# Sixths of the raw steps, halves of pair 0, and a swapped exponential: attention and a rational feed-forward layer on one core

## The chip, the core and the metric

The kernel runs on one core of one Trainium2 chip. A core has a matrix engine (PE, with its weight loads shown as PEld), a vector engine (DVE), a scalar engine (ACT), a general engine (POOL), an engine that issues most of the DMAs (SP), and 16 DMA engines. Each compute engine takes its own instructions strictly in order and waits on semaphores for the others. The metric is device microseconds (us) of one launch, the median over the runs; lower is better.

## What is computed

```python
scores = scale * q @ k.T                      # 4 batches x 12 heads, 448 tokens, head size 64, float32
scores = where(causal mask, scores, -1e9)
attn = exp(scores - rowmax);  attn /= sum(attn) + 1e-9
x = (attn @ v), heads side by side            # 1792 tokens x 768
h = x @ w_in                                  # w_in 768 x 2048, float64 in memory
g = (a0 + a1 h + a2 h^2 + a3 h^3) / (1 + |b0||h| + |b1| h^2 + 1e-6)
out = g @ w_out                               # w_out 2048 x 768, float64 in memory
```

The two weight matrices arrive as float64, so the kernel has to turn each 64-bit word into a float32 with integer operations.

## The kernel before

Two heads are handled together as one "pair"; there are 24 pairs, numbered 0 to 23, six to a batch. The loop over p runs from -1 to 23, and every turn works on several pairs at once: ORDER (lines 18 to 21) is a hand-written list of tasks, and `e.6@1` in it means task e, argument 6, for pair p-1. ORDER is the order in which instructions are put into each engine's queue. For one pair the tasks are: `ld` and `lv` (DMA loads of q, k and v, issued by SP), `qk` (PE transposes of q and k, line 296), `qx` and `qy` (copies of the two halves of rows out of PSUM, by ACT at line 311 and by DVE at 309 in the first pairs), `s` (scores, PE, line 328; s.0 makes block 0, and s.1, s.2 and s.3 make two blocks each), `m` (mask and row maximum, DVE, 339), `e` (exponential, ACT, 349; block 6 has 448 keys and block 0 has 64), `sm` and `r` (row sums on POOL, 356, reciprocal on DVE, 359), `n` (normalising, seven POOL operations, 366), `c` (PE transposes, 385), `a` and `v` (their copies by ACT, 395, and DVE, 397), `d` (attention times v, PE, 409), `dh` and `dl` (splitting the result into a high and a low part, ACT, and DVE at 437 or 439).

The conversion of weights is woven into this loop. A 128 x 768 piece ("raw" tile) m takes a POOL pass and then a DVE pass for each of two steps. In step 2, POOL copies the upper words (line 169, called by `cv.0`) and DVE shifts and ORs the lower words in (179). In step 3, POOL scales the upper words in place (173) and DVE shifts and ORs once more (185). `cv.0` stands near the start of a turn, behind POOL's last `n` of the turn before; the DVE pass, `cv.2`, stands at the end of a turn, behind DVE's last `m` and ahead of the `v` copies of the next turn. Before the change, pairs 3 to 15, 17, 19 and 21 each make one whole DVE pass of 768 columns (16 passes, eight pieces), with its POOL pass in the same turn. `quota` says how many steps a pair takes, and `conv` issues them.

At the start, matmuls on zeros (`keep_warm`, line 943, tile psI) fill PE until data come. After pair 23, a second hand-written list, TAIL, mixes the last attention work with the first feed-forward matmuls (`p1`, line 242, tile psH), whose PSUM banks are those of the closed score pool: the first psH tile takes the bank that pair 23's blocks 0 and 2 used. Then PE runs feed-forward work without a pause to the end. There too, DVE and POOL work side by side on weight pieces (lines 179, 185, 225, 525).

Of the kernel before, what the change touches and what calls it, by code (L numbers as in the profile page):

```python
# [17 lines left out]
ORDER = """  # L18
c.1@2 e.6@1 c.0@2 e.0@1 lv@-1 v.1@2 cv.0 dh@3 qk@-1 ld@-4 cv.3 a.1@2 sm@1 v.0@2 s.2 a.0@2 r@1 dl@3 qy@-1 n.2@1 s.3 qx@-1
n.3@1 m.3 m.4 s.0 n.5@1 s.1 e.3 m.5 d@2 n.0@1 e.4 n.4@1 m.0 e.5 m.1 n.6@1 m.2 e.1 m.6 n.1@1 e.2 cv.1 cv.2  # L20
# [7 lines left out]

FIRST = """
s.0 m.0 s.1 e.0 m.1 s.2 e.1 m.2 s.3 e.2 m.3 qk@-1 e.3 m.5 lv@-1 ld@-4 e.5 m.4 qy@-1 qx@-1 e.4 m.6 e.6  # L30
# [5 lines left out]
c.1@2 e.6@1 c.0@2 e.0@1 v.1@2 dh@3 a.1@2 xa.8 sm@1 xc.8.5 xa.9 v.0@2 a.0@2 r@1 co wl.0.0 xc.8.2 xc.8.3 xs.8 xd.11 xc.9.2  # L36
# [23 lines left out]
def kernel(  # L60
# [97 lines left out]
    def conv_step(m, s):  # L158
        raw = c_raw[m]
        yu = raw[:, :, 1]  # L160
# [11 lines left out]
        elif s == 5:  # L172
            nc.gpsimd.tensor_scalar(
                out=y, in0=y, scalar1=2.0 ** -112, scalar2=1.0, op0=ALU.mult, op1=ALU.mult
            )
        elif s == 4:
            nc.scalar.activation(out=y, in_=y, func=AF.Copy, scale=2.0 ** -112)
        elif s == 2:
            nc.vector.scalar_tensor_tensor(
                out=c_u[m], in0=raw[:, :, 0], scalar=29, in1=c_u[m],  # L180
                op0=ALU.logical_shift_right, op1=ALU.bitwise_or,
            )
        else:
            o = cv.tile([P, DM], F32, tag="ld", bufs=NL, name="w").bitcast(U32) if m < NL else c_u[m]
            nc.vector.scalar_tensor_tensor(
                out=o, in0=yu, scalar=3, in1=c_u[m], op0=ALU.logical_shift_left, op1=ALU.bitwise_or
            )
            c_32[m] = o.bitcast(F32)
# [65 lines left out]
    def stage_load(p):  # L254
# [33 lines left out]
    def qk_pe(p):  # L288
        ps = psa[p] = [ring(x, "psA") for x in range(2)]
# [9 lines left out]
        if p == 0:  # L299
            keep_warm(4)  # L300

    def qk_ev(p, x):
# [3 lines left out]
        o = QK[p].rearrange("p n (c r) -> p (n c) r", r=CP)[:, :, lo:hi]  # L306
        i = psa[p][x][:, :2 * NB * (hi - lo)].rearrange("p (c r) -> p c r", r=hi - lo)
# [139 lines left out]
    def conv(p, part):  # L447
        if part == 0:
            lo = sum(quota(x) for x in range(p))
            for m, n in steps[lo:lo + quota(p)]:  # L450
                conv_step(m, 1 if n == 2 else 5)
# [3 lines left out]
        else:  # L455
            lo = sum(quota(x) for x in range(p))
            mid, hi = lo + quota(p) // 2, lo + quota(p)
            for m, n in steps[lo:mid] if part == 1 else steps[mid:hi]:
                conv_step(m, n)
                if n == 3:  # L460
                    done.append(m)
# [3 lines left out]
        "qk": qk_pe, "qx": lambda p: qk_ev(p, 0), "qy": lambda p: qk_ev(p, 1),  # L465
# [5 lines left out]
    def parse(order):  # L471
# [9 lines left out]
        for order in (ORDER, FIRST, SECOND, THIRD)  # L481
# [411 lines left out]
    with tc.manual_schedule():  # L893
# [47 lines left out]
        def keep_warm(n):  # L941
            for _ in range(n):
                nc.tensor.matmul(idle, warm, warm, start=True, stop=True, skip_group_check=True)  # L943

        keep_warm(8)
# [6 lines left out]
        for p in range(NHEAD, NP):  # L952
# [4 lines left out]
            attend(p, begin[p] if 0 <= p < 3 else plan)  # L957
# [118 lines left out]
```

## Time and profile before

| What | Value |
|---|---|
| median of 3 runs | 602.48 us (602.44 to 602.89) |
| the profiled execution's own time | 602.94 us |
| its span, first to last instruction | 601.1 us |
| PE busy | 594.0 us, 99% of the span |
| DVE, ACT, POOL busy | 89%, 75%, 28% |
| chain that ended last: PE | 95% |

The span is what the trace shows, and the remaining 1.84 us lie around it. A busy engine in the table is one with an instruction in flight. The ends of matmuls are modelled, so that a PE that is busy all the time may still be held up a little by others. An instruction that waits inside the engine for something that is not a semaphore is shown as a longer instruction, not as idle time. So the length of a repeated stretch, and the length of one instruction beside its twins, tell more here than the busy shares.

### The profile page before, as it was taken

To read this page: it belongs to the slowest core of one execution; us is meant where nothing else is said; L and a number is where in the kernel's file an instruction comes from. 1 tells how busy PE (TensorE), PEld (TensorE's weight loads), DVE (VectorE), ACT (ScalarE), POOL (GpSimd) and SP (SyncE) were. 2 spreads that over 40 slices of the span, in tenths; PEclk is the share of its full clock that TensorE was granted. 3 is DMA by queue.
4 is the path that set the end of the run, shared out by engine and by line. 5 is a ranking of instruction groups with operands and counts; after the bars stand their busy time and mean duration, and the time that the engine had idled before them with its cause. 6 is when DMAs were issued, how large, how long until landed. Compare 5 with 4: busy or idle time off the path is not lost.

```text
span 601.1 us, 12762 instructions
## 1 busy us (share of the span) xinstructions
PE 594.0 (99%) x4660; PEld 494.2 (82%) x4660; DVE 535.9 (89%) x1015; ACT 448.6 (75%) x923; POOL 169.2 (28%) x266
## 2 busy tenths in 40 slices
PE   8999999999999999999999999999999999999997
PEld 6666666667888888888888888889999999998886
DVE  3999999988799999999999879998999999988950
ACT  4999999998877776668777776676477777677731
POOL 2899997766733401112333100000000000000000
PEclk9999999999999999999999999999999999999999
DMA  7979898776389988888985663443353344149872
GB/s 163 234 180 228 182 204 210 181 194 224 149 284 347 336 304 288 298 308 301 358 297 183 225 217 139 158 139 125 135 206 132 109 154 145 66 184 339 294 254 85
DMA packets 104863, 128.64 MB, mean 214 GB/s; under 512 B 70496, under 2 KB 82912, under 8 KB 104800
## 3 DMA queue, kind: packets, MB, share of 16 engines
q1 hardware_dynamic: 104800, 127.82, 67.2%
q8 instruction: 37, 0.61, 0.4%
q14 instruction: 26, 0.21, 0.1%
HBM read 98.31 MB, written 29.49 MB: 213 GB/s over the span
## 4 chain that ended last, share of the span: by engine, by line
PE 95%; DVE 2%; ACT 1%; POOL 1%; issue 0%; ACTq 0%
PE psO L614 25%; PE psH L242 22%; PE psQ L728 14%; PE psM L610 13%; PE psD L409 7%; PE psS L328 7%; PE psC L385 4%; PE psA L296 2%; PE psI L943 1%; ACT e L349 1%; POOL e L366 0%; DVE wq L707 0%; DVE xparts L637 0%; DVE p L528 0%; DVE at L397 0%
## 5 line engine op out<-in xcount | busy, mean ns | idle before, releaser
L614 PE MATMUL psO<-whl,gh 128*128 128x512 f32 x448 | 159.1, 391 | 0.0
L242 PE MATMUL psH<-xs,whl 128*128 128x512 f32 x576 | 136.7, 391 | 0.2 <-ACT e L349 0.2
L610 PE MATMUL psM<-whl,gh 128*128 128x256 f32 x448 | 126.2, 282 | 0.0
L242 PEld LDWEIGHTS psH<-xs,whl 128*128 128x128 f32 x576 | 105.9, 188 | 21.9 <-ACT e L349 0.3
L614 PEld LDWEIGHTS psO<-whl,gh 128*128 128x128 f32 x448 | 84.0, 188 | 17.8 <-ACT gh L540 0.4
L610 PEld LDWEIGHTS psM<-whl,gh 128*128 128x128 f32 x448 | 84.5, 189 | 1.7 <-DVE osb L598 0.3
L349 ACT ACTIVATE e<-psS,nm 128x448 f32<-128x448 f32 (+6 forms) x168 | 79.3, 568 | 4.3 <-DVE nm L339 3.2
L614 PE MATMUL psO<-whl,gl 128*128 128x512 f32 x224 | 81.1, 390 | 0.0
L728 PE MATMUL psQ<-xpart,wq 128*128 128x384 f32 x432 | 78.5, 336 | 0.1
L366 POOL TENSOR_SCALAR e<-e,r 128x192 f32<-128x192 f32 (+6 forms) x161 | 74.4, 487 | 13.9 <-DVE r L359 9.4
L728 PEld LDWEIGHTS psQ<-xpart,wq 128*128 128x128 f32 x432 | 74.8, 188 | 1.4 <-DVE hpair L754 0.4
L339 DVE CUSTOM_DVE_ANT_0 psS<-psS,mask 128x64 f32<-128x64 f32 (+6 forms) x168 | 65.4, 456 | 1.8 <-PE psS L328 1.3
L610 PE MATMUL psM<-whl,gl 128*128 128x256 f32 x224 | 63.2, 282 | 0.0
L169 POOL TENSOR_SCALAR u<-raw 128x768 f32<-128x768 f32 x32 | 36.9, 1153 | 57.6 <-DMA raw<-in_moe_w_out_dram 25.0
L517 ACT ACTIVATE w<-w 128x512 f32<-128x512 f32 x32 | 20.3, 633 | 39.8 <-DVE w L502 39.8
L614 PEld LDWEIGHTS psO<-whl,gl 128*128 128x128 f32 x224 | 42.0, 188 | 8.9
L328 PE MATMUL psS<-qkt 64*64 64x64 f32 (+6 forms) x672 | 47.5, 391 | 1.4 <-ACT e L349 1.2
L349 ACT ACTIVATION_READ_ACCUMULATOR e<-psS,nm 128x1 f32 x168 | 48.5, 299 | 0.0
L409 PE MATMUL psD<-at,vraw 128*64 128x448 f32 (+3 forms) x384 | 46.8, 386 | 0.0
L409 PEld LDWEIGHTS psD<-at,vraw 128*64 128x64 f32 x384 | 25.5, 136 | 24.9 <-issue 14.8
L610 PEld LDWEIGHTS psM<-whl,gl 128*128 128x128 f32 x224 | 42.3, 189 | 0.0
L328 PEld LDWEIGHTS psS<-qkt 64*64 64x64 f32 x672 | 21.3, 132 | 20.4 <-ACT at L395 10.7
(111 smaller groups left out, 1117.1 us busy)
## 6 DMA issues: line engine op xcount, KB each, us to landing
whl<-whl SPq DMA_DIRECT2D x64, 768.0 KB, 5.5
w<-w SPq DMA_DIRECT2D x51, 384.0 KB, 5.1
raw<-in_moe_w_in_dram SPq DMA_DIRECT2D x16, 768.0 KB, 5.4
raw<-in_moe_w_out_dram SPq DMA_DIRECT2D x16, 768.0 KB, 6.1
w<-u SPq DMA_DIRECT2D x26, 384.0 KB, 3.4
qraw<-in_q_dram SPq DMA_DIRECT2D x48, 112.0 KB, 3.5
kraw<-in_k_dram SPq DMA_DIRECT2D x48, 112.0 KB, 3.7
out_dram<-osb SPq DMA_DIRECT2D x13, 384.0 KB, 3.1
```

The costliest lines, as they stand in the source:

```text
L169: nc.gpsimd.tensor_scalar(out=u.bitcast(F32), in0=y, scalar1=0.0, scalar2=1.0, op0=ALU.mult, op1=ALU.mult)
L242: nc.tensor.matmul(ps, w[:, c * P:(c + 1) * P], xs[ck, part, c // K3][:, c % K3], start=(c == 0 and n == 0), stop=(c == KD - 1 and n == 2),)
L328: nc.tensor.matmul(pss[p, b][half((1 + b + j) % 2)], QK[p][half(j), 0, b * QB:(b + 1) * QB], QK[p][half(j), 1, :b_w[b]], start=True, stop= ...
L339: nc.vector.tensor_tensor_reduce(out=s, in0=s, in1=mask[:, S - w:], scale=-SCALE, scalar=3e38, op0=ALU.add, op1=ALU.min, accum_out=nmx[p][ ...
L349: nc.scalar.activation(out=E[p % 2][i][:, :w], in_=pss[p, i], func=AF.Exp, bias=nmx[p][:, i:i + 1], scale=-1.0, accum_out=SUM[p % 2][:, i: ...
L366: nc.gpsimd.tensor_scalar(out=e, in0=e, scalar1=REC[p][:, i:i + 1], scalar2=0.0, op0=ALU.mult, op1=ALU.add)
L385: nc.tensor.transpose(ps[x][:, slot // 2 * QB:(slot // 2 + 1) * QB], E[p % 2][n][r, lo:lo + P], ident[r, r])
L409: nc.tensor.matmul(ps[half(j), lo * QB:S], v[:, j, c], a[h][:, slot * QB:(slot + 7 - lo) * QB], start=(c == 0), stop=(c == 3), skip_group_ ...
L517: nc.scalar.activation(out=w, in_=w, func=AF.Abs)
L610: nc.tensor.matmul(acc["m", k], g, w[:, 512:], start=first and (k % 2 == 0 or each), stop=last, skip_group_check=True)
L614: nc.tensor.matmul(acc[k], g, w[:, :512], start=first, stop=last)
L728: nc.tensor.matmul(q_bank[j, bank], w[:, wp_, c * P:(c + 1) * P], xp_[:, c], start=(first and n == 0), stop=(n == 3 * K3 - 1), skip_group_ ...
```

## The change

It has three parts.

The raw steps are cut into sixths of 128 columns. A pair takes 5 sixths (pairs 3 to 12), 6 (13, 14, 15, 17, 19, 21), 4 (16) or 3 (18 and 20), 96 sixths in all for the same eight pieces. Sixths of the same step in one pair are joined into one DVE instruction, so a pair whose share crosses from one step into the next has two DVE instructions in a row where it had one. These are pairs 4, 5, 6, 7, 10, 11, 12, 13, 14, 15 and 19. POOL's pass is not cut: it is issued whole, at `cv.0` of the pair in which its step begins; only for the step that begins in pair 18 is it done by DVE, at `cv.2`, just ahead of that pair's 3 sixths.

Pair 0 is loaded, transposed and copied in two halves of 224 rows. The eight DMAs of q and k become halves, with q issued by SP and k by ACT; half 0 of both is transposed and copied, then block 0 of the scores is made, then half 1 is transposed and copied. The zero matmuls are 7 and, behind half 0, one of 128 and one of 64 columns, where there were 8, 2 and 4.

At the head of TAIL, the exponential of pair 23's block 0 (64 keys) is put ahead of that of block 6 (448 keys).

```diff
+ZEROTH = "lv@-1 qk.0@-1 ld@-4 qy.0@-1 qx.0@-1"
 FIRST = """
-s.0 m.0 s.1 e.0 m.1 s.2 e.1 m.2 s.3 e.2 m.3 qk@-1 ...
+s.0 m.0 qk.1 qx.1 qy.1 e.0 s.1 m.1 s.2 e.1 m.2 s.3 e.2 m.3 qk@-1 ...
 TAIL = """
-c.1@2 e.6@1 c.0@2 e.0@1 v.1@2 dh@3 a.1@2 ...
+c.1@2 e.0@1 c.0@2 e.6@1 v.1@2 dh@3 a.1@2 ...

-    def conv_step(m, s):
+    def conv_step(m, s, lo=0, hi=DM):
...
-        elif s == 5:
-            nc.gpsimd.tensor_scalar(
+        elif s in (5, 6):
+            (nc.gpsimd if s == 5 else nc.vector).tensor_scalar(
                 out=y, in0=y, scalar1=2.0 ** -112, scalar2=1.0, op0=ALU.mult, op1=ALU.mult
             )
...
-                out=c_u[m], in0=raw[:, :, 0], scalar=29, in1=c_u[m],
+                out=c_u[m][:, lo:hi], in0=raw[:, lo:hi, 0], scalar=29, in1=c_u[m][:, lo:hi],

     def stage_load(p):
...
-            for j in range(2):
-                nc.sync.dma_start(out=t[:, :, j], in_=src[b, 2 * hp + j].rearrange("(c p) d -> p c d", p=CP))
+            eng, nh = (nc.scalar if n == "k" else nc.sync, 2) if p == 0 else (nc.sync, 1)
+            for h in range(nh):
+                for j in range(2):
+                    x = src[b, 2 * hp + j].rearrange("(c p) d -> p c d", p=CP)
+                    cs = slice(h * NB // nh, (h + 1) * NB // nh)
+                    eng.dma_start(out=t[:, cs, j], in_=x[:, cs])

-    def qk_pe(p):
+    def qk_pe(p, h=None):
...
-            if p == 0 and n == 1:
-                keep_warm(2)
-            for c in range(NB):
+            for c in cols_of(h):
...
-        if p == 0:
-            keep_warm(4)
+        if h == 0:
+            keep_warm(1)
+            keep_warm(1, QB)

+    NQ = 6
     def quota(p):
-        return int(3 <= p < 16 or p in (17, 19, 21))
-    steps = [(m, n) for m in range(NC) for n in (2, 3)]
+        if 3 <= p < 13:
+            return 5
+        if p in (13, 14, 15, 17, 19, 21):
+            return 6
+        return {16: 4, 18: 3, 20: 3}.get(p, 0)
+    steps = [(m, n, i) for m in range(NC) for n in (2, 3) for i in range(NQ)]

     def conv(p, part):
+        now = steps[lo:lo + quota(p)]
         if part == 0:
+            for m, n, i in now:
+                if i == 0 and p != 18:
+                    conv_step(m, 1 if n == 2 else 5)
...
+        elif part == 2:
+            runs = {}
+            for m, n, i in now:
+                runs.setdefault((m, n), []).append(i)
+            for (m, n), r in runs.items():
+                if p == 18:
+                    conv_step(m, 6)
+                conv_step(m, n, r[0] * DM // NQ, (r[-1] + 1) * DM // NQ)

-        keep_warm(8)
+        keep_warm(7)
```

## Rows read from the trace of the kernel before

**Rows 1.** The page's part 1: busy us (share of the span) and instructions by engine.

```profile
PE 594.0 (99%) x4660; PEld 494.2 (82%) x4660; DVE 535.9 (89%) x1015; ACT 448.6 (75%) x923; POOL 169.2 (28%) x266
```

**Rows 2.** Busy time by stretch, one turn each: stretch, length, PE, PEld, DVE, ACT, POOL.

```profile
31.13:36.60 5.47, 5.47 (x95) 3.48 (x96) 5.47 (x20) 5.47 (x21) 4.98 (x10) 1.00 1.07 222
...
53.02:58.57 5.55, 5.55 (x94) 3.53 (x96) 5.55 (x22) 5.55 (x21) 5.05 (x10) 1.00 0.75 202
...
102.49:107.88 5.39, 5.39 (x94) 3.50 (x96) 5.33 (x20) 5.39 (x21) 3.33 (x9) 1.00 0.99 189
107.88:113.27 5.39, 5.39 (x94) 3.62 (x96) 4.47 (x20) 5.39 (x20) 4.38 (x10) 1.00 0.70 155
```

**Rows 3.** Timeline (start, length, engine, line, tiles): one split operation, then turn 10's end.

```profile
24.09 0.57 DVE L437 TENSOR_TENSOR xs<-psD,xs 128x448 fp32r<-128x448 f32 x1
...
65.82 1.08 DVE L185 SCALAR_TENSOR_TENSOR u<-raw,u 128x768 uint32<-128x768 uint32 x1
...
66.06 1.62 POOL L169 TENSOR_SCALAR u<-raw 128x768 f32<-128x768 f32 x1
...
68.13 0.64 DVE L437 TENSOR_TENSOR xs<-psD,xs 128x64 fp32r<-128x64 f32 x2
```

**Rows 4.** Timeline of DVE and POOL, where two DVE operations meet a POOL pass.

```profile
139.03 0.94 DVE L225 TENSOR_TENSOR whl<-w,whl 128x768 fp32r<-128x768 f32 x1
139.05 1.66 POOL L169 TENSOR_SCALAR u<-raw 128x768 f32<-128x768 f32 x1
139.89 1.63 DVE L179 SCALAR_TENSOR_TENSOR u<-raw,u 128x768 uint32<-128x768 uint32 x1
...
142.50 0.95 DVE L179 SCALAR_TENSOR_TENSOR u<-raw,u 128x768 uint32<-128x768 uint32 x1
```

**Rows 5.** Timeline around the end of turn 18, and a one-input DVE operation.

```profile
109.88 0.93 POOL L169 TENSOR_SCALAR u<-raw 128x768 f32<-128x768 f32 x1
...
110.47 1.29 DVE L397 COPY at<-psC 128x512 f32<-128x512 f32 x2 [0.92 <-PE psC L385]
...
131.10 0.56 DVE L217 CAST whl<-w 128x768 fp32r<-128x768 f32 x1
```

**Rows 6.** Timeline of the head.

```profile
0.74 0.93 SPq L262 DMA_DIRECT2D qraw<-in_q_dram  x2
...
1.11 3.78 PE L943 MATMUL psI<-e 128*128 128x128 f32 x16 [1.11 <-DVE e L939]
...
4.82 0.69 PE L296 MATMUL psA<-ident,qraw 64*128 64x64 f32 x8
...
5.44 1.22 PE L943 MATMUL psI<-e 128*128 128x128 f32 x4
...
7.31 0.59 ACT L311 COPY qkt<-psA 128x512 f32<-128x512 f32 x1 [5.30 <-PE psA L296]
...
8.51 1.95 PE L328 MATMUL psS<-qkt 64*64 64x64 f32 x28
...
10.53 0.57 DVE L339 CUSTOM_DVE_ANT_0 psS<-psS,mask 128x384 f32<-128x384 f32 x1 [0.24 <-PE psS L328]
```

**Rows 7.** The zero matmuls of two stretches: ns min/median/max, first and last start.

```profile
L943 PE MATMUL psI<-e x4: 421/421/580, 5.4 to 6.2; 128*128 128x128 f32 x4
...
L943 PE MATMUL psI<-e x6: 275/275/275, 7.5 to 8.1; 128*128 128x128 f32 x6
```

**Rows 8.** DMAs into qraw in the first 8 us: time from issue to landing.

```profile
DMA to landing us min/median/max: 2.4/3.2/3.5
```

**Rows 9.** Chain of waits, pieces in order of time (start, length, what): the head's end.

```profile
17.06 1.18 PE psC L385 x28
```

**Rows 10.** Timeline of the tail's begin.

```profile
136.71 0.66 ACT L349 ACTIVATE e<-psS,nm 128x448 f32<-128x448 f32 x1
...
137.32 0.34 ACT L349 ACTIVATE e<-psS,nm 128x64 f32<-128x64 f32 x1
...
137.80 3.97 PEld L242 LDWEIGHTS psH<-xs,whl 128*128 128x128 f32 x18 [0.31 <-ACT e L349]
```

More of the change, by code (lines that the diff above doesn't have):

```diff
@@ L286, in ring, with cols_of @@
         return (ps_s if n == 3 else ps_t).tile([P, 512], F32, tag=f"x{n}", name=name)
-    def qk_pe(p):
-        ps = psa[p] = [ring(x, "psA") for x in range(2)]
+    def cols_of(h):
+        return range(NB) if h is None else range(2 * h, 2 * h + 2)
+    def qk_pe(p, h=None):
+        if p not in psa:
+            psa[p] = [ring(x, "psA") for x in range(2)]
+        ps = psa[p]
         for n, src in enumerate(("q", "k")):
-            if p == 0 and n == 1:
-                keep_warm(2)
-            for c in range(NB):
+            for c in cols_of(h):
                 for x, w in enumerate((QB, CP - QB)):
@@ L305, in qk_ev @@
         lo, hi = x * QB, (QB, CP)[x]
-        o = QK[p].rearrange("p n (c r) -> p (n c) r", r=CP)[:, :, lo:hi]
-        i = psa[p][x][:, :2 * NB * (hi - lo)].rearrange("p (c r) -> p c r", r=hi - lo)
+        if h is None:
+            o = QK[p].rearrange("p n (c r) -> p (n c) r", r=CP)[:, :, lo:hi]
+            i = psa[p][x][:, :2 * NB * (hi - lo)].rearrange("p (c r) -> p c r", r=hi - lo)
+        else:
+            cs = slice(cols_of(h).start, cols_of(h).stop)
+            o = QK[p].rearrange("p n (c r) -> p n c r", r=CP)[:, :, cs, lo:hi]
+            i = psa[p][x][:, :2 * NB * (hi - lo)].rearrange("p (n c r) -> p n c r", n=2, r=hi - lo)[:, :, cs]
         if p == 3 or p < 3 and x == 1:
@@ L439, in d_lo @@
                 nc.vector.tensor_copy(out=o, in_=ps[:, r])
+    NQ = 6
     def quota(p):
-        return int(3 <= p < 16 or p in (17, 19, 21))
-    steps = [(m, n) for m in range(NC) for n in (2, 3)]
+        if 3 <= p < 13:
[4 more added lines that the diff above has]
+    steps = [(m, n, i) for m in range(NC) for n in (2, 3) for i in range(NQ)]
     done = []
     def conv(p, part):
+        lo = sum(quota(x) for x in range(p))
+        now = steps[lo:lo + quota(p)]
         if part == 0:
-            lo = sum(quota(x) for x in range(p))
-            for m, n in steps[lo:lo + quota(p)]:
-                conv_step(m, 1 if n == 2 else 5)
+            for m, n, i in now:
+                if i == 0 and p != 18:
+                    conv_step(m, 1 if n == 2 else 5)
         elif part == 3:
@@ L454, in conv @@
                 conv_load(done.pop(0) + NR)
[L455 to L460, printed above, removed]
+        elif part == 2:
[6 more added lines that the diff above has]
+                conv_step(m, n, r[0] * DM // NQ, (r[-1] + 1) * DM // NQ)
+                if n == 3 and r[-1] == NQ - 1:
                     done.append(m)
@@ L480 @@
         [(fn, arg, lag or 0) for fn, arg, lag in parse(order)]
-        for order in (ORDER, FIRST, SECOND, THIRD)
+        for order in (ORDER, ZEROTH, FIRST, SECOND, THIRD)
     )
@@ L939, with keep_warm @@
         nc.vector.memset(warm, 0.0)
-        def keep_warm(n):
+        def keep_warm(n, w=P):
             for _ in range(n):
-                nc.tensor.matmul(idle, warm, warm, start=True, stop=True, skip_group_check=True)
-        keep_warm(8)
+                nc.tensor.matmul(idle[:, :w], warm, warm[:, :w], start=True, stop=True, skip_group_check=True)
+        keep_warm(7)
         def attend(p, part):
```

22 lines of the change are left out of this document (12 added, 10 removed).

## The prediction

> **What bounds the kernel now.** I read the page's first part, then a table of the attention loop turn by turn, then timelines of DVE and POOL. PE is busy for 99% of the span [rows 1], so time can be won only where PE is held up: in the head, where little runs side by side; in turns that last longer than PE needs; and at the step into the feed-forward work. The reader should see in the table that turns 17 and 18 last 5.39 us, the one with a whole DVE pass in it and the other without [rows 2]. That is PE's own pace. Turns 3 to 14 last 5.44 to 5.55 us, and DVE is then busy all the time, as in turns 4 and 8 [rows 2]: there DVE is the bound. Over the 13 turns from 3 to 15 the excess over 5.39 adds up to some 1.5 us, which is all that a better spread could give back.
>
> The timeline of turn 10's end shows something that busy shares hide. DVE begins its pass at 65.82, POOL comes to its own pass at 66.06, and POOL's pass is 1.62 us long [rows 3], where one without a DVE pass beside it takes 0.93 [rows 5]. The two engines exclude each other. Later rows show the other side: DVE begins an operation on two SBUF operands at 139.03, POOL's pass comes up at 139.05, DVE's next such operation is due at 139.89 and takes 1.63 us, where a lone one takes 0.95 [rows 4]. So POOL waits for the first, then goes before the second, and the second waits 1.63 - 0.95 = 0.68 us. I counted ten places between 139 and 267 us where a POOL pass of this kind comes up under such a DVE operation with another right behind it; the second was lengthened in all ten, and no POOL pass waited for both. This decides the forecast, since the change puts two DVE passes in a row where there was one.
>
> The Trainium skill, in "SBUF — State Buffer", section "SBUF: two separate sides", has a rule that speaks against this change: DVE, when it reads two SBUF operands, and POOL, when it reads SBUF, share a pair of ports, and whoever starts first holds it for its whole instruction. By that rule the wait could be as long as the POOL pass itself, 0.93 us, and the sum below would be some 2.2 us higher. The trace agrees in kind, and its wait is 0.68.
>
> **The change part by part: the sixths.** Durations: cutting one DVE operation of 448 columns in two costs 0.64 - 0.57 = 0.07 us [rows 3], so I take 0.07 as the fixed part. A whole pass alone is 0.95 [rows 4]; a sixth is then (0.95 - 0.07) / 6 = 0.147. Five sixths cost 0.80 in one operation and 0.87 in two; six in two cost 1.02.
>
> Where DVE is the bound, its own sum is the turn. Turns 3, 8 and 9 take five in one operation: 0.15 less each, which brings 5.55 to about PE's 5.39 or 5.40, together -0.45. Turn 7 takes five in two, but turn 8 begins no step, so no POOL pass comes up: -0.08.
>
> Turns 4, 5, 6, 10, 11 and 12 take five in two, and 13 and 14 six in two, and in the turn behind each of these a step begins. Its POOL pass stands right behind POOL's last normalising operation, and that ends just after DVE's pass begins (65.82 against 66.06 [rows 3]; it is so in each of these turns). POOL's pass will therefore come up under the first of the two operations and go before the second: +0.68 each. Turns with five: 0.68 - 0.08 = +0.60, six times, 3.6. Turns with six: 0.68 + 0.07 = +0.75, twice, 1.5. Behind the waiting operation on DVE stand the `v` copies of the next turn, then `r`, `dl` and the `m`. PE's score matmuls wait for the banks that the `v` copies free, and the exponentials for `m`. In these turns DVE has no idle time that could take it.
>
> Turns 15 and 19 take six in two with no POOL pass behind: 0.07 each, partly in DVE's last slack, together +0.05. Turn 16's four sixths and turn 20's three fall into idle time of DVE. Turn 18 has 0.92 us of it, ahead of the copies [rows 5]. There DVE gets a scaling of 768 strided columns, priced between the 0.56 of a one-input operation of this size [rows 5] and the 0.95 of a two-input one [rows 4], half a pass (0.51), and the wait for POOL's pass between them, 0.68: 1.75 to 2.14, less 0.92, that is +0.8 to +1.2, and I take +1.0. What it takes away is a POOL pass of turn 18, which hid beside other work.
>
> Sum of this part: -0.45 - 0.08 + 3.6 + 1.5 + 0.05 + 1.0 = +5.6. Bounds: turns 4 and 10 have a first operation of one sixth only, 0.22 us, which may be over before POOL asks (-0.68 each), and turn 18 may cost nothing: +3.2. With waits as long as the POOL pass (0.93) in nine places it is +7.9.
>
> **The halves.** Eight zero matmuls took 3.78 us [rows 6], so seven end at about 4.4. Loads of q land 2.4 to 3.5 us after their issue, the median 3.2 [rows 8], and an SP issue takes 0.47 [rows 6]; half 0 of q and k, issued from 0.74 as two and two, lands by about 1.2 + 3.2 = 4.4, at the same moment. That ACT issues a DMA as fast as SP is not in the trace; if each took twice as long, half 0 would land near 5.4, +1.0. ACT's table load, now behind four issues, ends near 4.0, before its first copy. Eight transposes take 0.69 [rows 6]: 5.1. One and a half zero matmuls at 0.45 to 0.6 (two took 1.22 [rows 6]) end near 5.85, the shorter copies near 5.5, so block 0 starts at about 5.9 instead of 8.51. Eight more transposes: 6.75. Half 1's copies, shorter than the 0.59 of a whole one [rows 6]: 7.15. So s.2 starts at about 7.2. Before, all scores of pair 0 took 1.95 us [rows 6]; s.0 and s.1 are 384 of their 1792 columns, so s.2 started 0.42 behind 8.51, at 8.93. That is 1.7 earlier, and the same for the wait of DVE for the last scores, which ended at 10.53 [rows 6]. From there the chain runs through exponentials, sums and POOL to PE's first big transposes at 17.06 [rows 9] with the same steps as before: -1.7. Bounds: -2.6 if half 1 stays off the path, 0 if the clock (below) comes late.
>
> **The swap.** The first psH matmul starts at 137.80, its weight load having waited 0.31 for block 0's exponential, which started at 137.32 behind the one of 448 keys [rows 10]. In the new order it ends about 0.6 earlier, and PE is then held by its transposes: -0.25 (0 to -0.3). The row sums wait for both exponentials anyway.
>
> **Sum.** 602.94 + 5.6 - 1.7 - 0.25 = 606.6 for the profiled execution. The median of the runs shown is 0.46 below it, so I predict 606.1.
>
> **The rivals.** First, no turn is taken: the second DVE operation is already queued and follows at once. For it speaks that the two are short and of one kind; against it the ten places. Then turns 4, 5, 6, 10, 11 and 12 give 0.08 each, 13 and 14 cost 0.07 each, 18 about 0.3: -0.45 - 0.08 - 0.48 + 0.14 + 0.05 + 0.3 = -0.5, and with head and tail 602.48 - 2.45 = 600.0. This one ends on the other side, faster; it decides from the point where fewer than three or so of the nine waits happen. Second, the clock. The granted clock of the rows is 1.00 throughout, yet the zero matmuls' passes took 421 ns until 6.6 us and 275 ns from 7.2 on [rows 7], the lower and the higher of the two levels, 1.2 and 2.4 GHz; before the rise PE was fed without a gap from 1.11. The change takes out five and a half of 14 zero matmuls. If the rise came only behind pair 0's scores, s.1 to s.3 would take some 1.5 us longer and the head's gain would be 0.2: 607.6. The Trainium skill, in "TensorE: Matmul & The Clock Gate", Part 4, says that transposes don't bring the clock up, which leans that way; no row here separates it. Third, the waits come but fewer or shorter (turns 4 and 10 free, 18 cheap): 602.48 + 3.2 - 1.95 = 603.7, and lower if the first operation no longer waits for POOL: about 603.
>
> **How the numbers follow.** The forecast has 0.60 (606.1, its own range 604.0 to 607.8), no turn 0.20, the late clock 0.10, the few waits 0.10. A difference of 0.2%, 1.2 us, is about what a measurement of this kernel can tell from no change. Faster than 601.3: the first rival, 0.20. Within 0.2%: most of the third, 0.09. Slower than 603.7: the rest, 0.71. The range of 600.0 to 607.8 takes half of the first rival, all of the third and nearly all of the others.
>
> **What would show it.** In turns 4 to 6 and 10 to 14 the second of two DVE passes (lines for 179 and 185) should be about 0.7 us longer than its columns ask, with POOL's pass ending just before its end, and these turns should last 6.1 to 6.3 us, turns 3, 7, 8 and 9 about 5.4, turn 18 about 6.4. Block 0 should start near 5.9 and the first big transposes near 15.4. If the long passes are absent I was wrong about the turns; if block 0 starts near 5.9 but the transposes near 17, about the head.

## The result and the profile after

The changed kernel takes 608.01 us, median of 5 runs (607.68 to 609.27), beside 602.54 us (602.44 to 602.89) for the kernel before: a ratio of 1.010, 95% interval 1.0089 to 1.0112. (Ratios, here and below, are worked out over all runs of both kernels and need not be the quotient of the two medians.) It is slower, as forecast, by 1.9 us more than forecast and 0.2 us beyond the end of the range. The profiled execution took 608.01 us, with a span of 606.2 against 601.1.

The page's part 1 of the kernel after (busy us, share, instructions), which answers to [rows 1]:

```profile
PE 597.7 (99%) x4650; PEld 495.6 (82%) x4650; DVE 544.0 (90%) x1031; ACT 449.6 (74%) x924; POOL 168.2 (28%) x265
```

It hides everything: PE is 99% busy in both, though it does ten matmuls less. The turns tell more. Busy time by stretch of the kernel after, as in [rows 2], each stretch from one turn's first `psD` matmul to the next one's: turns 5, 6, 9, 11, 13 and 18.

```profile
35.70:41.82 6.12, 6.08 (x95) 3.80 (x93) 6.12 (x21) 5.56 (x19) 4.63 (x10) 1.00 0.62 136
41.82:47.97 6.15, 6.08 (x95) 3.81 (x93) 6.15 (x21) 5.56 (x19) 4.66 (x10) 1.00 0.64 144
...
59.34:64.86 5.52, 5.52 (x94) 3.48 (x92) 5.33 (x21) 5.52 (x21) 4.76 (x10) 1.00 1.04 261
...
70.51:76.64 6.13, 6.13 (x94) 3.80 (x92) 6.13 (x22) 5.62 (x20) 4.63 (x10) 1.00 0.77 168
...
82.80:89.08 6.28, 6.15 (x95) 3.81 (x93) 6.28 (x22) 5.62 (x20) 4.79 (x10) 1.00 0.87 186
...
112.14:118.03 5.89, 5.87 (x94) 3.66 (x93) 5.68 (x20) 5.07 (x19) 4.40 (x9) 1.00 0.61 128
```

Turns 5, 6, 11 and 12, with five sixths in two operations, last 6.12 to 6.16 us, and 13 and 14, with six, 6.27 to 6.28, where before they lasted about 5.5. The wait stands at the end of a turn and lengthens mostly the next one: the first of each run, turns 4 and 10, lasts 5.78 and 5.65, and turns 7 and 15, behind the last, still last 5.62 and 5.75. The timeline of DVE and POOL in the kernel after (start, length, engine, line) shows why: the ends of turns 4 and 11, and turn 18.

```profile
31.63 0.47 DVE L181 SCALAR_TENSOR_TENSOR u<-raw,u 128x128 uint32<-128x128 uint32 x1
31.92 0.96 POOL L171 TENSOR_SCALAR u<-raw 128x768 f32<-128x768 f32 x1
32.02 1.41 DVE L189 SCALAR_TENSOR_TENSOR w<-raw,u 128x512 uint32<-128x512 uint32 x1
...
72.66 0.54 DVE L181 SCALAR_TENSOR_TENSOR u<-raw,u 128x256 uint32<-128x256 uint32 x1
72.89 1.07 POOL L171 TENSOR_SCALAR u<-raw 128x768 f32<-128x768 f32 x1
73.12 1.26 DVE L189 SCALAR_TENSOR_TENSOR u<-raw,u 128x384 uint32<-128x384 uint32 x1
...
114.02 0.56 DVE L175 TENSOR_SCALAR raw<-raw 128x768 f32<-128x768 f32 x1
114.13 1.22 POOL L171 TENSOR_SCALAR u<-raw 128x768 f32<-128x768 f32 x1
114.61 1.15 DVE L189 SCALAR_TENSOR_TENSOR u<-raw,u 128x384 uint32<-128x384 uint32 x1
```

POOL's pass comes up under the first DVE operation, goes before the second, and the second is 1.41 us long. 512 columns alone take 0.68 (the fence of `e4_apart` below), so the wait is 0.73. It is the picture of [rows 4], and it stands in all nine places the forecast named, also where the first operation is one sixth, as at turn 4's end.

The head of the kernel after, answering to [rows 6, 9]: block 0's first scores, SyncE's issue of pair 3's `k`, its transposes, the first big transposes.

```profile
6.01 0.33 PE L345 MATMUL psS<-qkt 64*64 64x64 f32 x4
...
10.07 1.02 SPq L270 DMA_DIRECT2D kraw<-in_k_dram  x2
...
15.20 0.45 PE L307 MATMUL psA<-ident,kraw 64*128 64x64 f32 x8 [1.33 <-DMA kraw<-in_k_dram]
15.47 1.18 PE L402 MATMUL psC<-ident,e 64*128 64x64 f32 x32
```

Block 0 starts at 6.01 instead of 8.51. All 32 big transposes start at 15.47; before, four of them stood at 15.67 and 16.23, and 17.06 was the start of the other 28. But PE stands 1.33 us before pair 3's `k`. Two things come together there. The load is issued at 10.07, as before (10.02), since SyncE issues load after load without a pause from 0.74 us on. And it lands later, first in the kernel after, then in the one before:

```profile
DMA to landing us min/median/max: 4.5/4.6/4.7
DMA to landing us min/median/max: 2.9/3.0/3.1
```

In the kernel before, it had landed at 13.67 us. PE was ready for it at 13.87 in the kernel after (15.20 less 1.33), so with the landing time of before it would not have waited. The wait is handed on: DVE's copies of these transposes and POOL's normalising, which stands behind the reciprocal `r`, start 0.88 and 0.96 us earlier than before, not 1.7. After, then before:

```profile
15.69 1.16 DVE L326 COPY qkt<-psA 128x384 f32<-128x384 f32 x2 [0.63 <-PE psA L307]
18.24 3.19 POOL L383 TENSOR_SCALAR e<-e,r 128x192 f32<-128x192 f32 x7 [1.83 <-DVE r L376]
...
16.57 1.14 DVE L309 COPY qkt<-psA 128x384 f32<-128x384 f32 x2
19.20 3.21 POOL L366 TENSOR_SCALAR e<-e,r 128x192 f32<-128x192 f32 x7 [1.14 <-DVE r L359]
```

Why the load lands late isn't shown. Of the 19 traces of this document that issue it there, it took 3.6 us or more in nine, and these are the nine in which an instruction load of 0.02 MB begins at 12.54 us or earlier; in the ten in which that one begins later, it took 3.13 us or less. No run moves the instruction load.

The tail's begin, which answers to [rows 10]:

```profile
141.97 0.33 ACT L366 ACTIVATE e<-psS,nm 128x64 f32<-128x64 f32 x1
...
142.81 1.42 PE L246 MATMUL psH<-xs,whl 128*128 128x512 f32 x5
```

PE's wait of 0.31 us for the exponential is gone.

Below, "lead" is how much earlier a turn's first `psD` matmul starts than in the trace of before (20.05 us in turn 2, 25.51 in turn 3, and so on). After had a lead of 1.54 us in turn 2, 0.98 in turn 3, a lag of 0.50 in turn 7, 4.11 in turn 16, 5.28 in turn 21 and 5.01 in turn 25.

### The profile page after: what moved, and what is told of

Same layout as the page of the kernel before. It is cut to its first block, busy times and chain, and to the rows that moved or that the text cites. A ratio compares the mean times of both kernels' runs of the same rounds, so it can differ in the third digit from the quotient of the medians.

```text
span 606.2 us, 12764 instructions
## 1 busy us (share of the span) xinstructions
PE 597.7 (99%) x4650; PEld 495.6 (82%) x4650; DVE 544.0 (90%) x1031; ACT 449.6 (74%) x924; POOL 168.2 (28%) x265
## 4 chain that ended last, share of the span: by engine, by line
PE 83%; DVE 10%; issue 2%; ACT 2%; DVEq 0%; ACTq 0%
PE psO L642 25%; PE psH L246 22%; PE psQ L756 14%; PE psM L638 13%; PE psD L426 4%; PE psS L345 3%; DVE psS L356 3%; PE psC L402 2%; ACT e L366 1%; DVE at L414 1%; DVE u L181 1%; DVE nm L356 1%; PE psA L307 1%; DVE u L189 1%; DVE w L189 1%
## 5 line engine op out<-in xcount | busy, mean ns | idle before, releaser
L366 ACT ACTIVATE e<-psS,nm 128x448 f32<-128x448 f32 (+6 forms) x168 | 77.9, 509 | 9.5 <-DVE nm L356 5.2
L345 PE MATMUL psS<-qkt 64*64 64x192 f32 (+6 forms) x672 | 51.7, 391 | 1.5 <-ACT e L366 0.8
L345 PEld LDWEIGHTS psS<-qkt 64*64 64x64 f32 x672 | 23.9, 132 | 23.0 <-DVE at L414 8.6
L181 DVE SCALAR_TENSOR_TENSOR u<-raw,u 128x768 uint32<-128x768 uint32 (+5 forms) x39 | 41.8, 1071 | 0.0
```

The costliest lines, as they stand in the source:

```text
L181: nc.vector.scalar_tensor_tensor(out=c_u[m][:, lo:hi], in0=raw[:, lo:hi, 0], scalar=29, in1=c_u[m][:, lo:hi], op0=ALU.logical_shift_right, ...
L345: nc.tensor.matmul(pss[p, b][half((1 + b + j) % 2)], QK[p][half(j), 0, b * QB:(b + 1) * QB], QK[p][half(j), 1, :b_w[b]], start=True, stop= ...
L366: nc.scalar.activation(out=E[p % 2][i][:, :w], in_=pss[p, i], func=AF.Exp, bias=nmx[p][:, i:i + 1], scale=-1.0, accum_out=SUM[p % 2][:, i: ...
```

## The experiments

**The parts alone.** My theory: each place where two DVE passes follow each other with a POOL pass beside costs some 0.7 us, and the sixths are the whole loss. The halves alone (passes whole, old tail), the sixths alone, and the kernel before with every whole pass cut in two halves in its place:

```
# e1_halves: the changed kernel with
return 6 * int(3 <= p < 16 or p in (17, 19, 21))   # quota, and the old TAIL
# e2_sixths: the kernel before with conv_step, quota, steps and conv of the changed one
# e3_cut: the same, quota as in e1_halves, and in conv
-    conv_step(m, n, r[0] * DM // NQ, (r[-1] + 1) * DM // NQ)
+    for x in range(2):
+        conv_step(m, n, x * DM // 2, (x + 1) * DM // 2)
```

> Only the halves of pair 0 are added to the kernel before; the raw steps stay whole and the exponentials in their old order. Theory: half 0 and block 0 bring the head 1.6 us forward, and then pair 3's k, whose DMAs SP issues no earlier than before, holds PE up, so that about 1.0 us is left at turn 3 and kept to the end: 601.5 us (601.0 to 602.0). Rival, that the head's gain is given back later in turns that DVE bounds: 602.3 to 602.7. My prediction's own term, -1.7: 600.8.

> Only the sixths are added to the kernel before; head and tail are the old ones. Theory (POOL's pass takes its turn between two DVE operations in nine turns, 0.6 to 1.0 us each): 602.5 + 6.3 = 608.8 us (607.8 to 609.5), with the second operation of turns 4, 5, 6, 10 to 14 some 0.7 us longer than its columns ask. Rival, that the loss comes from the earlier head meeting later loads: near 603.

> The kernel before with its old shares, but each whole DVE pass of the raw steps in pairs 3 to 21 is cut into two of 384 columns, one right behind the other. Nothing else is changed, and no work is moved to another turn. Theory: in turns 3 to 14 a POOL pass comes up under the first and goes before the second, 0.68 + 0.07 us each, 12 times: 602.5 + 9.0 = 611.5 us (610 to 612.5), while turns 15, 17, 19 and 21, behind which no POOL pass follows, hardly change. Rival, that a cut costs only its fixed part and the loss came from where the sixths lie: 12 x 0.07 = 0.8 us, 603.3 us.

Measured beside 602.37 us for before: the sixths 609.14 us (ratio 1.0111, 1.0090 to 1.0133), the cut passes 611.46 (1.0148, 1.0128 to 1.0169), both as my theory had them; nothing is moved in `e3_cut`, and it is the slowest of the three. The halves took 603.52 (1.0019, 1.0009 to 1.0028), where I expected a gain: a miss, taken up below.

**The second operation elsewhere.** The changed kernel, with the second of two operations moved behind the `v` copies:

```
-sm@1 v.0@2 s.2
+sm@1 v.0@2 cv.4@1 s.2        # cv.2 issues the first operation, cv.4 the others
```

> The changed kernel, with the second DVE operation of a pair moved behind the two v copies of the next turn, which read PSUM; in pair 18 the half pass moves behind them too. The work is the same, only the place of the second operation differs, so that POOL's pass runs beside the copies. Theory: the second operations take no longer than their columns ask, turns 4 to 6 and 10 to 12 last 5.4 to 5.45 us, 13 and 14 about 5.6, turn 18 at most 0.5 more than 5.39: 601 us (600.3 to 602.3). Rival, that two operations cost as much wherever they stand, or that the copies' delay was not the path: 606 to 608 us.

604.36 us (1.0031, 1.0019 to 1.0042): most of the loss is gone, so it hung on the two operations standing together. But it is 3.4 us above what I expected. Timeline of turn 4's end in `e4_apart`:

```profile
31.74 0.49 DVE L181 SCALAR_TENSOR_TENSOR u<-raw,u 128x128 uint32<-128x128 uint32 x1
32.05 0.97 POOL L171 TENSOR_SCALAR u<-raw 128x768 f32<-128x768 f32 x1
32.57 1.29 DVE L414 COPY at<-psC 128x512 f32<-128x512 f32 x2 [0.34 <-PE psC L402]
...
33.77 0.68 DVE L189 SCALAR_TENSOR_TENSOR w<-raw,u 128x512 uint32<-128x512 uint32 x1
```

The DVE copies, which read PSUM, run beside POOL's pass without waiting, and the 512 columns take 0.68.

**Is it POOL's pass?** `e3_cut`, with POOL's exponent pass (every second turn's) shortened to 32 columns; the weights are not the reference's.

```
+    z = y[:, :32]
-    out=y, in0=y, scalar1=2.0 ** -112, ...
+    out=z, in0=z, scalar1=2.0 ** -112, ...
-    op0=ALU.logical_shift_left, ...      # step 3; unscaled values would overflow
+    op0=ALU.logical_shift_right, ...
```

> The kernel with every whole pass cut 3 + 3 (611.46 us), with GpSimd's exponent pass shortened from 768 columns to 32; GpSimd's other pass, in every second turn, keeps its 768. The shift of the third step goes right instead of left, for the same time, since unscaled values would overflow; the weights are not the reference's. My theory, a GpSimd pass that waits takes its turn between two VectorE operations and the second waits for it to end: the turns whose cut pass stands beside the short one fall from 6.3 to 5.5 or 5.6 us, the others stay at 6.3; 6 or 7 turns by 0.65 us, so 607.2 us (606.5 to 608.2). Rival, cutting a pass costs its 0.7 us whatever GpSimd does (the second operation must wait for the first one's writes, or for anything but GpSimd): all cut turns stay at 6.3 us and the time at 611.5.

607.31 us (1.0077, 1.0060 to 1.0095), as my theory had it. Timeline (start, length) of a turn with the long and of one with the short POOL pass, DVE's two operations in one row each:

```profile
43.99 1.92 DVE L188 SCALAR_TENSOR_TENSOR w<-raw,u 128x384 uint32<-128x384 uint32 x2
44.28 1.23 POOL L169 TENSOR_SCALAR u<-raw 128x768 f32<-128x768 f32 x1
...
50.27 1.22 DVE L180 SCALAR_TENSOR_TENSOR u<-raw,u 128x384 uint32<-128x384 uint32 x2
50.56 0.51 POOL L174 TENSOR_SCALAR raw<-raw 128x32 f32<-128x32 f32 x1
```

The two DVE operations take 1.92 us beside the long pass, 1.22 beside the short one, and the turns alternate, for instance these two:

```profile
41.95:48.18 6.23, 6.03 (x96) 3.81 (x92) 6.23 (x21) 5.54 (x19) 4.74 (x10) 1.00 0.65 156
48.18:53.80 5.62, 5.62 (x94) 3.99 (x92) 5.62 (x21) 5.58 (x20) 3.95 (x10) 1.00 1.19 248
```

So the price is POOL's pass, not the cut.

**The tail, the halves again, and earlier loads.** `e5_tail` is the kernel before with the new TAIL order alone; `e6_early_loads` is `e1_halves` with pair 3's loads ahead of pair 0's `v`:

```
-ZEROTH = "lv@-1 qk.0@-1 ld@-4 qy.0@-1 qx.0@-1"
+ZEROTH = "ld@-4 lv@-1 qk.0@-1 qy.0@-1 qx.0@-1"
```

> The kernel before with only the order of pair 23's two softmax pieces changed (64 keys ahead of the 448). My theory: the 0.33 us piece ends 0.6 us earlier than the 448 keys' did, and the wait of 0.2 to 0.3 us at the first column matmul goes: 602.37 - 0.2 = 602.2 us (602.0 to 602.4). Rival, the matmul has something else to wait for and nothing moves: 602.4. The trace's head is that of the kernel before, so it also shows how far that head varies from one execution to the next: block 0's first score matmul at 7.2 to 7.5 us as in the two kernels that cut the passes without the halves, or at 8.5 as in the profiled execution of before.

> The halves alone, a second time, as the control for the next kernel: 603.5 us (602.8 to 604.0). Its trace should show the first score matmul at 5.4 to 6.3 us and again a wait of about 1 us of pair 3's k transposes for their load, at 14 to 15 us; if its later turns wait for k loads too, as one did at 55 us in the first trace, then the gain is given back to the loads, and if they don't, something else makes this kernel's median longer.

> The halves alone, with pair 3's q and k issued ahead of pair 0's v on SyncE. Theory one, the head ends at pair 3's k, whose issue at 10.1 us stands behind pair 0's v: the issue comes at 8.2 us, the wait of 1.3 us at the k transposes goes, and the time falls by 0.9 us (0.5 to 1.3) against the halves alone, to about 602.6 us. Theory two, all loads of the first 60 us come at the pace of the DMA queues (engines 86% busy), so that what is moved ahead makes another load late: no change, 603.5 us, and a wait appears at pair 0's v or at a later pair's k.

The tail: 601.94 us beside 602.49 (0.9994, 0.9985 to 1.0004). Too little for the runs to tell from nothing, but in the trace the lead grows from 0.27 us in turn 23 to 0.53 in turn 24. The halves again: 602.76 (1.0002, 0.9989 to 1.0015). Earlier loads: 603.33 (1.0006, 0.9995 to 1.0018); pair 3's `k` transposes start at 13.93 us, and the next step, the big transposes, now waits for POOL: nothing gained, theory two by the time. In the trace, though, its lead of 1.39 us in turn 2 is kept (1.40 in turn 3), while the six traces with a long wait for this `k` lose 0.28 to 1.10 us there: in the head the wait did cost that, and the median doesn't show it.

In after, `e1_halves` both times, `e4`, `e6` and `e10` the halves' lead in turn 2 is 1.4 to 2.1 us, and it melts in three places: at pair 3's `k` (a wait of 0.9 to 1.5 us in six of the eleven traces with the new head: after, five of `e1_halves`, `e4`, `e6`, `e10`, `e12`, `e15`); at the first weights, for which POOL waits 0.2 to 1.6 us at 21 to 23 us in five traces with halves; and in turn 13, below. The old head is not free of the first two: `e2` and `e3`, the two of its traces that reach turn 2 earliest (18.78 and 18.96 us), wait 0.51 and 0.26 us for the weights and 0.35 and 0.41 for a `k`. So it may be the early head that meets these loads, not the halves as such; no run tests that.

**Another place for the pass.** `e9_behind` is `e5_tail` with the whole passes moved behind the `v` copies, where they shouldn't meet POOL's pass; `e10_behind_halves` adds the halves.

```
-ld@-4 cv.3 a.1@2 sm@1 v.0@2 s.2 ... n.1@1 e.2 cv.1 cv.2
+ld@-4 a.1@2 sm@1 v.0@2 cv.1@1 cv.2@1 cv.3 s.2 ... n.1@1 e.2
```

> The tail's change, and every whole VectorE pass moved from ahead of the copies of the transposed softmax to behind them, one turn later, so that it no longer stands beside GpSimd's pass. My theory: which of the two passes comes first decides, and behind the copies they do not meet, so GpSimd's pass takes 0.93 us instead of 1.62 in all turns and VectorE's never 1.72; turns fall from 5.5 towards the 5.39 of the turns without a pass, by 0 to 0.1 us in 13 turns: 602.4 - 0.25 - 0.6 = 601.5 us (600.8 to 602.3). Rival: the pass in its new place delays the masks of the next scores, as the second operation did where it stood behind the copies (turns 8 to 12 gained nothing, three others lost 0.3): 602.3 to 604 us.

> The same with the halves of pair 0. In the traces of the halves a lead of 1.1 to 1.8 us at pair 6 fell to 0.2 to 0.9 us, most of it in the turns after one in which GpSimd's pass came 0.01 to 0.3 us ahead of VectorE's, which then took 1.72 or 1.40 us instead of 1.07. Theory one, the halves' gain is lost to that order of the two passes: with the passes apart it stays, and this kernel is 1.1 us (0.8 to 1.5) below the one beside it, about 600.4 us. Theory two, the gain is lost to the loads of the first 60 us: within 0.4 us of the one beside it.

610.47 us beside 602.61 for before (1.0132, 1.0115 to 1.0149): a clear miss. The passes don't meet any more (0.95 and 0.93 us), but all turns with a pass last 6.0 us. Timeline of `e9_behind`, the lines of the kernel before:

```profile
39.84 1.29 DVE L397 COPY at<-psC 128x512 f32<-128x512 f32 x2 [0.55 <-PE psC L385]
41.05 0.95 DVE L179 SCALAR_TENSOR_TENSOR u<-raw,u 128x768 uint32<-128x768 uint32 x1
41.91 0.19 DVE L359 RECIPROCAL r<-r 128x7 f32<-128x7 f32 x1
42.28 0.89 POOL L366 TENSOR_SCALAR e<-e,r 128x192 f32<-128x192 f32 x2 [1.58 <-DVE r L359]
```

The reciprocal stands behind the pass, POOL waits 1.58 us for it, PE's big transposes wait for POOL, and DVE's copies for PE (0.55 us): a ring of 6.0 us. `e4_apart` put its second operation into the same place, and in its long turns, as 5 and 12, POOL waits up to 1.0 us for the reciprocal; its trace goes from a lead of 1.10 us in turn 3 to a lag of 0.82 in turn 25. That this is what it lacks is not shown; I have not tried it apart from that. `e10_behind_halves` took 610.81 (1.0136, 1.0120 to 1.0152), 0.34 above its neighbour, which is theory two by the time; its trace keeps a lead of 1.3 us over the other from turn 3 to the end, which is theory one. But the profiled run of `e10_behind_halves` is the fastest of its four (609.50) and that of `e9_behind` the slowest of its four (610.78), so the 1.3 us say little of the medians. Four runs don't settle it.

**Whole passes beside a short POOL pass,** without and with the halves (the edit of `e8_short_pool` on the kernel before and on `e1_halves`):

> The kernel before, passes whole and in their place, with GpSimd's exponent pass shortened from 768 columns to 32 (the weights are not the reference's; the third step shifts right for the same time). In the kernel before VectorE's pass comes first in all eleven turns, so the other's length costs nothing: 602.4 us (601.9 to 602.7). If the time falls by more than 0.5 us, GpSimd's pass is on the path in some executions of the kernel before too. It is the base of the next kernel.

> The halves alone, with the same short exponent pass: the turns where GpSimd's exponent pass came first (at 59 and 82 us in the traces of the halves) can no longer cost VectorE 0.3 to 0.7 us. Theory one, the halves' gain is lost to the order of the two passes: 0.9 us (0.5 to 1.5) below the kernel beside it. Theory two, it is lost at the loads (the wait of 1.0 to 1.3 us for pair 3's k and the later ones): within 0.4 us of it.

602.21 us (1.0001, 0.9991 to 1.0011) and 602.76 (1.0009, 0.9999 to 1.0019). The first fits: POOL's pass, when it comes second, is off the path. The second says that the order of the passes is not all. Its trace shows something else in the head. Timeline, pair 0's later scores in `e12_short_pool_halves`:

```profile
7.31 3.06 PE L345 MATMUL psS<-qkt 64*64 64x192 f32 x24
```

and in `e1_look4`:

```profile
6.19 2.15 PE L345 MATMUL psS<-qkt 64*64 64x192 f32 x24
```

The same 24 matmuls take 1.42 times as long in `e12_short_pool_halves`, as the zero matmuls of [rows 7] did before the rise (1.53 times), with a granted clock of 1.00 in the rows of both. The first transposes that run fast start at 10.30 us there, and turn 2's first `psD` is 0.58 us later than in `e11_short_pool_whole`.

**More zero matmuls, and three single executions.** `e13_more_zeros` is `e1_halves` with four zero matmuls behind half 0 instead of one and a half (`keep_warm(4)`); `e1_look3`, `e1_look4` and `e1_look5` are one execution each of `e1_halves` itself, with its trace.

> The halves alone, with four zero products instead of one and a half between pair 0's first half and its first block, as many as the kernel before issues there. Theory one, the rise of TensorE's speed: in one of seven traces with halves the scores of pair 0 ran at the slower speed (24 products in 3.06 us instead of 2.15), and the head ended 0.6 us later than that of the kernel before instead of 1.2 us earlier; more zero products keep TensorE busy until the rise, so the scores are fast in every execution, the first at 6.3 to 7.2 us, and the time is 0.4 to 1.0 us below the halves' 602.8 to 603.5, about 602.2 us. Theory two, the loads take the gain: 602.8 to 603.5 us, as the halves.

> The halves alone, one look, for the spread of its head: the 24 score products of pair 0 in 2.15 us and the first product with v at about 18.0 us (theory one's fast case: 602.1 us or less), or in 3.06 us and at about 19.9 us (its slow case: 603 us or more). Theory two: the time follows the waits for k loads at 10, 14 and 30 to 60 us, whatever the scores.

> As the look before it, another execution: theory one, fast scores go with 602.1 us or less and slow ones with 603 us or more; theory two, the time follows the waits for k loads.

> As the two looks before it, another execution: theory one, fast scores go with 602.1 us or less and slow ones with 603 us or more; theory two, the time follows the waits for k loads.

603.13 us beside 601.98 (1.0022, 1.0010 to 1.0035), and 603.11, 603.82 and 603.68 for the three executions. Theory one falls as the explanation of the median: the scores of `e13_more_zeros` run fast, its lead in turn 13 is 1.30 us, as hoped, and in turn 16 it is 0.55. Of the three executions two had fast scores and one (`e1_look5`) slow ones, and the time doesn't follow. `e1_look3` shows a second effect of the waits for loads. Busy time by stretch, the last columns granted clock, DMA share and GB/s; ahead of this stretch PE had waited 0.38 us for `q` and 0.82 for `k`:

```profile
11.06:14.66 3.60, 3.60 (x33) 1.75 (x32) 2.25 (x8) 2.02 (x8) 2.83 (x7) 0.53 0.70 155
```

The granted clock is 0.53, the lower level, and pair 1's scores take 3.60 us instead of 2.03.

All three executions, too, lose 0.74 us between turns 13 and 16. Timeline of `e1_look5`, masks and passes of turn 13 (the expectations below call it turn 11, counted from the first turn with a `psD`):

```profile
81.17 0.14 DVE L356 DVE_READ_ACCUMULATOR2_ANT nm<- 128x1 f32 x1
81.45 0.30 DVE L356 CUSTOM_DVE_ANT_0 psS<-psS,mask 128x128 f32<-128x128 f32 x1
...
82.55 0.93 POOL L175 TENSOR_SCALAR raw<-raw 128x768 f32<-128x768 f32 x1
82.56 0.14 DVE L356 DVE_READ_ACCUMULATOR2_ANT nm<- 128x1 f32 x1
82.56 1.71 DVE L181 SCALAR_TENSOR_TENSOR u<-raw,u 128x768 uint32<-128x768 uint32 x1
```

DVE pauses 0.28 us between two masks, where the next one otherwise starts with the read at 81.17. It comes to its whole pass 0.01 us behind POOL, and now DVE waits: 1.71 us instead of 1.05. This stands in six of the seven traces with halves, whole passes in their old place, the full POOL pass and no added memsets; the seventh has it at 59 us instead, behind a wait for `k`.

**Whose pause is it?** DVE has 1016 instructions with the halves and 1015 before. So I added tiny memsets to DVE's idle head: one to the kernel before, 18 to `e1_halves`.

```
 nc.vector.memset(warm, 0.0)
+for _ in range(1):                    # 18 in e15_eighteen_memsets
+    nc.vector.memset(lnb[:, 0:1], QC * 2.0 ** -LSH)
```

> The kernel before with one more tiny VectorE instruction in its idle head (a repeated memset of one column, 0.06 us), as many instructions on VectorE as the kernel with halves (1016 against 1015). In all traces with halves VectorE pauses 0.1 to 0.27 us between two masks of turn 11, and in all but one GpSimd's pass then comes first and VectorE's takes 1.72 us instead of 1.05, which costs 0.74 us over three turns; in the traces of the old head the pause is about 0.1 us one mask later and VectorE's pass comes first by 0.2 us. Theory one, the pause belongs to a place in VectorE's instruction stream, and one instruction more moves it: the long pause and the 1.72 us appear here too, and the time rises by 0.7 us, to 603.0 us. Theory two, it comes with what the halves change in the loads or in the time: no pause, 602.3 us.

> The halves alone, with 18 such memsets in VectorE's idle head. Theory one, the pause moves 18 instructions earlier in the stream, ahead of the reciprocal that GpSimd waits for too, so VectorE and GpSimd are late alike: VectorE's pass of turn 11 comes first, 1.05 us, and of the 0.74 us some 0.5 to 0.74 come back: 602.3 us where the halves had 602.8 to 603.5. Theory two: pause and 1.72 us stay at turn 11, 603.0 us.

602.79 us (1.0000, 0.9991 to 1.0009) and 603.02 (1.0003, 0.9993 to 1.0013), beside 602.59. Timeline of turn 13 in `e14_one_memset`:

```profile
81.19 0.14 DVE L339 DVE_READ_ACCUMULATOR2_ANT nm<- 128x1 f32 x1
81.39 0.30 DVE L339 CUSTOM_DVE_ANT_0 psS<-psS,mask 128x128 f32<-128x128 f32 x1
...
82.50 0.95 DVE L179 SCALAR_TENSOR_TENSOR u<-raw,u 128x768 uint32<-128x768 uint32 x1
82.59 1.65 POOL L173 TENSOR_SCALAR raw<-raw 128x768 f32<-128x768 f32 x1
```

and in `e15_eighteen_memsets`:

```profile
81.55 0.14 DVE L356 DVE_READ_ACCUMULATOR2_ANT nm<- 128x1 f32 x1
81.55 0.33 DVE L356 CUSTOM_DVE_ANT_0 psS<-psS,mask 128x128 f32<-128x128 f32 x1
...
82.69 1.09 DVE L181 SCALAR_TENSOR_TENSOR u<-raw,u 128x768 uint32<-128x768 uint32 x1
82.95 1.62 POOL L175 TENSOR_SCALAR raw<-raw 128x768 f32<-128x768 f32 x1
```

With one memset the pause stands where the halves have it, 0.20 us long, but DVE still comes first by 0.09 us and nothing is lost: the pause moved as theory one said, the 0.7 us I expected with it didn't come. With 18 the pause is gone from this place, DVE's pass takes 1.09, and the lag is 0.43 us in turn 13 and 0.44 in turn 16. That fits a pause at a place in DVE's instruction stream: in `e14_one_memset` and in the halves' traces the late mask is the same one in number, the 262nd from 0. But the number alone doesn't decide. In `e15_eighteen_memsets` the 262nd (at 76.27 us) starts without delay, and no such pause stands elsewhere, so theory one had the order right and its reason is not shown; in `e10_behind_halves` the same mask of turn 13 has the same number and starts without delay. What makes the pause stays open. The median of `e15_eighteen_memsets` didn't fall as I expected, and its trace is one with slow scores (24 in 3.47 us).

No kernel of these beats the one before by more than the runs can tell.

## Why the prediction was wrong in size and right in kind

Direction and mechanism held; the sum was too low. On the profiled executions it gave 606.6 and 608.01 were measured, 1.4 us more; the other 0.5 us of the miss is the median: before, the profiled run lay 0.46 above its median, and I took that off, but the profiled run of after lies on its median. Such an offset belongs to one execution and should not be carried over.

- **Two passes with POOL's between, +0.60 and +0.75 each: right.** From one DVE pass to the next (start to start, against before) turns 4, 5 and 6 grew by 0.65, 0.63 and 0.63, 10 to 12 by 0.66, 0.61 and 0.61, 13 and 14 by 0.82 and 0.75: 5.36 us where I had 5.1. The rule of the Trainium skill, "SBUF — State Buffer", section "SBUF: two separate sides", that an engine holds the shared ports for a whole instruction, is borne out: `e8_short_pool` shows that the wait goes with POOL's length. By that rule I gave 0.93 us as an upper price; the runs show 0.73 in turn 4, 0.71 in turn 11 (1.26 less the 0.55 of 384 columns alone in `e4_apart`) and 0.70 between the turns of `e8_short_pool`, for POOL's pass is under way before the second operation is due.
- **One pass of five sixths, -0.15 in turns 3, 8 and 9: partly wrong.** They gave -0.12, -0.17 and +0.12; with turn 7 as forecast, turns 3 to 14 came to +5.11 instead of +4.57.
- **Turns 15 and 19, +0.05 together: too low.** The lag grew by 0.20 us from turn 15's pass to turn 17, and by 0.09 in 19; the cut passes were not hidden.
- **Turn 18, +1.0: nearly right.** +0.86; the scaling took 0.56 (so DVE's one-input price held on strided columns) and the wait came.
- **The halves, -1.7: the step that failed.** Block 0 started at 6.01 (5.9 forecast) and the big transposes at 15.47 (15.4): both held, though in the kernel before the first four big transposes stood at 15.67 and 16.23, ahead of the 17.06 that the term counts from. What failed is "From there the chain runs ... with the same steps as before". A second chain, the loads, joins the first: pair 3's `k` is issued at 10.07 us whatever pair 0 does, it landed 4.5 to 4.7 us later instead of 2.9 to 3.1, and it held PE for 1.33 us. DVE's copies of it had a lead of 0.88, POOL's normalising behind them 0.96, and turn 3 the 0.98 that was left: 0.72 us of the 1.4. Most of the other half is the turns' 5.11 for 4.57 and the 0.24 of turns 15 and 19, above; turn 18 and the swap change it by less. Whether this `k` lands late differs from trace to trace, for a reason that isn't shown, so the size of that half is in part luck.
- **And the term was measured against one execution.** Over eight traces with the old head (this one, `e2`, `e3`, `e5`, `e8`, `e9`, `e11`, `e14`) turn 3's first `psD` starts at 24.24 to 25.51 us, mean 24.99; over the eleven with the new at 23.83 to 25.83, mean 24.67. The halves gain 0.3 us there, less than either spread, and I priced them from one of the two slowest traces of the old head. In the old head the moment differs from which PE is fast: eight transposes of pair 0 take 0.46 us at 4.53 in `e2`, whose block 0 starts at 7.26, and 0.69 at 4.82 and 0.68 at 6.59 in the kernel before, whose block 0 starts at 8.51. The trace that I priced is one where PE became fast late.
- **The swap, -0.25: right** where it is alone (0.26 in `e5_tail`), 0.18 in the changed kernel.
- **The rivals.** "No turn is taken" and "few waits" are excluded by the nine waits. "The clock" is no account of this trace, where four transposes take 0.47 us at 4.40 and 0.34 at 6.27, so that PE is fast from then on; but it does happen: the scores of pair 0 ran slow in three of the eleven traces with the new head (`e12`, `e15`, `e1_look5`) and in none of the eight with the old. That transposes don't bring the clock up, which I cited from the Trainium skill ("TensorE: Matmul & The Clock Gate", Part 4), no run here tells apart.
- **What stays open:** why the halves alone come out no faster. Two medians lie 1.15 and 0.27 us above that of before (the second can't be told from none), and the three executions 1.1 to 1.8 us. The traces show four takers, each measured in some of them: waits for `k`, the wait for the first weights, 0.74 us in turn 13 behind the pause, slow scores in three of eleven. Behind the head they account for the traces: of the seven with halves, whole passes in place, the full POOL pass and no added memsets, five fall back by 0.66 to 0.93 us from turn 3 to turn 25, and the two with the longest wait for the first weights (0.87 and 1.61 us) by 1.25 and 1.55; where DVE comes first in turn 13 (`e15`) it is 0.08, and with the short POOL pass (`e12`) none is lost. Whether they account for the medians isn't shown: taking out one of them (earlier loads, a short POOL pass, more zeros, the pause moved) never brought the median below that of before, and no run takes out all.

## What to carry to other kernels

Two VectorE operations on SBUF operands in a row are one operation too many where a GpSimd pass can come up under the first: the second then waits for the rest of the GpSimd pass, some 0.7 of its 0.93 us here, so an operation is better left whole, or its parts put so that GpSimd is not due between them, and not ahead of anything for which GpSimd waits. A price for a start that was read from one execution should be held against several, and before a gain in a head is counted, the issue and landing times of the loads that come next should be followed too, over several traces: where they don't move with it, the gain can end there.

## What I had not expected of the hardware

Which of the two passes comes first is decided by hundredths of a microsecond, and it matters: GpSimd second costs nothing here (its pass takes 1.62 us, and `e11_short_pool_whole`, which shortens every second one, gains nothing), GpSimd first by 0.01 us costs VectorE 0.66 us, and the kernel, with the pause ahead of it, 0.74. VectorE pauses 0.20 to 0.28 us ahead of one mask of turn 13 in the traces of the halves; one more instruction at its start brought such a pause into the kernel before, 18 more took it out of the halves. Its cause is open: instruction loads of 0.02 MB come every 6 to 10 us all along, but in `e1_look5` the one nearest starts at 82.9 us, behind the pause. The load of pair 3's `k` took 3.6 to 4.7 us in nine traces and 3.13 or less in ten, split by whether an instruction load began by 12.54 us, which is a coincidence of times that no run has tested. And a wait of TensorE for loads, 0.38 and 0.82 us, was followed by a granted clock of 0.53 for 3.6 us.
